# One-token attention and a gated MLP on one core: result, gate and pieces of x as eight neighbouring rows, and wo's last four rows through masked stationary tiles

## The chip, the cores and the metric

The kernel runs on one core of a Trainium2 chip. The metric is the device time of one execution in microseconds (us); smaller is better. Of several executions the median is given.

## The reference

Two tokens (B = 2, one position each, D = 512) go through an attention block with a cached K and V, and through an MLP whose output gates the attention's:

```
xn = _layernorm(x, axis=-1)
q = (xn @ wq).reshape(B, 1, 32, 128).transpose(0, 2, 1, 3)
scores = einsum("bhqd,bhkd->bhqk", q, k_cache) * 128 ** -0.5     # 8192 keys
o = einsum("bhqk,bhkd->bhqd", softmax(scores), v_cache)
s = o.transpose(0, 2, 1, 3).reshape(B, 1, 4096) @ wo
h = _gelu(_layernorm(xn) @ w1 + b1)                              # 512 -> 1376
g = _silu(h @ w2 + b2)                                           # 1376 -> 512
out = x + s * g
```

Everything is float32. K and V are 268 MB each; wq and wo have 8.4 MB each, w1 and w2 2.8 MB each.

## The kernel before

Each engine runs its own program, written out in the order of the code, with semaphores between them. The helper `op` (line 51) records nearly every instruction, so the profile shows L51 for nearly all. Names such as `bank` and `big` stand for all of PSUM's eight banks and for the three large SBUF buffers; most of the weights of the setup lie in the third of these.

**Transfers.** SP issues almost all of them on one queue: w2's tail, w1, wq, the first K tile, w2, the second K tile, x as `x4`, the first V tile, then K and V tiles in turn (32 pairs of 8.4 MB tiles). The first V tile overwrites the setup's weights, so SP waits for the setup's last matmul (`pgate`, line 304) ahead of it. At the end `wo` comes into the last V buffer in seven pieces (`WO_CUTS`: wo rows 0-9, 10-17, 18-23, 24-27, 28-29, 30 and 31, where a "row" c is one [128, 512] block), the last of them in two halves of the columns.

**Loop.** For each of the 32 tiles VectorE (DVE) multiplies K by q and sums, ScalarE (ACT) makes the exponentials, and TensorE (PE) multiplies them with V. Some matmuls with `ident` (the helper `unread`) write results that nobody reads.

**The end.** The normalised attention output lies in `on`: column c of it, for the B = 2 tokens, is the stationary operand for row c of wo. In the kernel before `on` is [128, 17, 32], zero except in the entries 0 and 16 of the 17, so that a matmul writes 17 neighbouring partitions and the two tokens come 16 partitions apart. Rows 0 to 27 are "wide": all 512 columns in one matmul, with c modulo 4 choosing one of four strips of 32 PSUM partitions in `pw`. ACT then copies `pw` to `o4`, and four matmuls with `mod` (a 0/1 matrix) add the four strips into `acc`. Rows 28 to 31 go straight into `acc`: the 512 columns are cut into QT = 4 quarters of 128, and quarter j goes to the strip 32j of `acc`, with one matmul per row and quarter. So `acc`, `gate`, `x4` and `res` are [128, 128], with useful rows at 32j + 16b. DVE makes `res = 0.5 * acc * gate + x4` in two instructions, and SP writes `res` out from eight partitions, 16 apart. PE reaches the rows in the order 0 to 29, then the four matmuls with `mod`, then 30 and 31.

In the setup, four matmuls (`pgate`) bring the gate's input into the same layout, with `mod_b` as the stationary tile and one strip for each quarter. `pqa` is another part of the setup that the prediction speaks of: eight matmuls with 64 stationary columns each and 128 moving columns, all into the same 64 partitions of one bank.

Of the kernel before, what the change touches and what calls it, by code (L numbers as in the profile page):

```python
# [5 lines left out]
ALU = mybir.AluOpType  # L6
# [7 lines left out]
class Program:  # L14
# [32 lines left out]
    def op(self, eng, method, *args, waits=(), sig=None, by=1, quiet=False, **kwargs):  # L47
        need = self.need(eng, waits)
        for name, v in need[:-1]:
            self.engines[eng].wait_ge(self.sem(name), v)  # L50
        ins = getattr(self.engines[eng], method)(*args, **kwargs)  # L51
        for name, v in need[-1:]:
            ins._wait_ge(self.sem(name), v)
        if quiet:
            return None
        name = sig or "own_" + eng
        by = 16 if method == "dma_start" else by
        ins.then_inc(self.sem(name), by)
        self.counts[name] += by
        return name, self.counts[name]  # L60


def decode_kernel(nc, x, kc, vc, wq, wo, w1, b1, w2, b2, out):
    P = 128
    B, H, S, DH = kc.shape
# [10 lines left out]
    SCALE = float(DH) ** -0.5  # L76
    QT = 4
    R = P // QT
    HB = R // B
    MB = HB * (B - 1) + 1  # L80
    JW = 512 // DH
    NT = KP // JW
    NF = F // P
# [3 lines left out]
    OC = DH // PH  # L87
# [4 lines left out]
    WIDE = 28  # L92
# [3 lines left out]
    op, wait, take = pr.op, pr.wait, pr.take  # L96

    def sb(shape, name):
        return nc.alloc_sbuf_tensor(name, list(shape), F32).ap()
# [30 lines left out]
    g_nat = boot(P, D)  # L130
    wq_sb = big[1].rearrange("p (c n) -> p c n", n=H * DH)
    wo_sb = big[2].rearrange("p (c n) -> p c n", n=D)
# [6 lines left out]
    mod = sb([P, R], "mod")  # L139
# [3 lines left out]
    mine = sb([BH, N], "mine")  # L143
    side = sb([BH, U], "side")
    sides = sb([BH, P], "sides")
    x4 = sb([P, P], "x4")
    gate = sb([P, P], "gate")
    res = sb([P, P], "res")
    z = sb([P, P], "z")
    th = sb([P, P], "th")  # L150
    xnT = sb([P, ND, B], "xnT")
    yT = sb([P, ND, B], "yT")
    hT = sb([P, NF + 1, B], "hT")
# [8 lines left out]
    o4 = sb([P, JW * DH], "o4")  # L162
# [1 line left out]
    Z = sb([P, BH, PH], "Z")  # L164
    ZL = sb([P, N, U * PH], "ZL")
    rl = sb([P, B], "rl")
    on = sb([P, MB, OC], "on")
    mod_b = sb([P, R], "mod_b")

    bank = [ps([P, 512], f"bank{i}") for i in range(8)]  # L170
    po = bank[0]
    pm = bank[1]
    pn = bank[2]
    pt = bank[3]
    acc = bank[4][:, :P]
    OA = bank[5][:, :B * (OC + 1)].rearrange("p (b c) -> p b c", c=OC + 1)
    pg = bank[6]
    pw = bank[1]
    ph = bank[7][:, :NH * P]
    pgate = bank[7][:, :P]  # L180
    phT = bank[3][:, R:R + (NF + 1) * B]
    PQ = [bank[1], bank[2]]
    pxn, py = bank[3][:, :ND * B], bank[5][:, :ND * B]
# [9 lines left out]
    def pe_n(name, n):  # L193
        return name, n + 1

    t = {}
# [19 lines left out]
    a = op("POOL", "memset", ident, 0.0)  # L216
# [2 lines left out]
    t["sel0"] = op("POOL", "memset", sel, 0.0)  # L219
    op("POOL", "memset", PZ, 0.0)  # L220
    op("POOL", "memset", srow, SCALE)
    t["x4m"] = op("POOL", "memset", x4, 0.0)
    t["on0"] = op("POOL", "memset", on, 0.0)
    a = op("POOL", "memset", mod_b, 0.0)
    t["pool"] = op("POOL", "memset", gate, 0.0)
    op("DVE", "memset", eps_t, EPS)
    for k in (7, 6, 1, 2, 4, 0):
        t[f"mem{k}"] = t["mem"] = op("DVE", "memset", bank[k], 0.0)
# [3 lines left out]
    a = op("DVE", "tensor_reduce", out=side, in_=pairs.rearrange("h n s -> h s n"), axis=AX.X, op=ALU.add)  # L232
    t["side"] = op("DVE", "tensor_copy", sides.rearrange("h (s r) -> h s r", r=HP),
                   side.unsqueeze(2).to_broadcast([BH, U, HP]), waits=[a])
    a = op("DVE", "tensor_reduce", out=half1, in_=ident.rearrange("p (s r) -> p s r", s=U), axis=AX.X, op=ALU.add)
    t["half"] = op("DVE", "tensor_copy", half.rearrange("p (s r) -> p s r", r=PH),
                   half1.unsqueeze(2).to_broadcast([P, U, PH]), waits=[a])
    t["mod"] = op("DVE", "tensor_reduce", out=mod, in_=by_row, axis=AX.X, op=ALU.add, waits=[t["ident"]])
    t["mod_b"] = op("DVE", "tensor_copy", mod_b[:, ::HB], mod[:, :B], waits=[t["mod"], t["pool"]])
    t["blk"] = op("DVE", "tensor_reduce", out=blk, in_=ident.rearrange("p (j r) -> p j r", r=R), axis=AX.X,  # L240
                  op=ALU.add)
    t["sel"] = op("DVE", "tensor_copy",
                  sel[:, HP:].rearrange("p (b j r) -> p b j r", b=B, r=HG)[:, :, :QT, 0], by_row[:, :B, :],
                  waits=[t["sel0"]])
# [22 lines left out]
    a = op("DVE", "tensor_copy", gh, phT.rearrange("p (f b) -> p f b", b=B), waits=[pe("phT")])  # L267
    c = op("DVE", "tensor_mul", gu, gh, gh, waits=[a])
    c = op("DVE", "tensor_scalar", gu, gu, GELU_A, 1.0, op0=ALU.mult, op1=ALU.add, waits=[c])
    c = op("DVE", "tensor_mul", gu, gu, gh, waits=[c])  # L270
    c = op("ACT", "activation", gu, gu, AF.Tanh, scale=GELU_C, waits=[c])
    c = op("DVE", "scalar_tensor_tensor", gu, gu, 1.0, gh, op0=ALU.add, op1=ALU.mult, waits=[c])
# [8 lines left out]
    for part, n0, n1 in (("first", 0, NPB), ("rest", NPB, N)):  # L281
        shape = [BH, n1 - n0, DH]
        t[f"QN {part}"] = op("DVE", "tensor_tensor", out=QN[:, n0:n1, :], in0=q_all.unsqueeze(1).to_broadcast(shape),
                           in1=mine[:, n0:n1].unsqueeze(2).to_broadcast(shape), op=ALU.mult,
                           waits=[t["qall"], t["mine"]])

    for g in range(N // NPB):
        last = {"sig": "s_q", "by": NPB // U * (2 if g == QH + 1 else 1)} if g != QH else {}
# [7 lines left out]


    load_k(1, pe("pq"), ("d_wq", 16))
    for b in range(B):
        t["x4"] = op("SP", "dma_start", x4[HB * b::R, :], x[b, 0].rearrange("(j n) -> j n", n=P), sig="d_x4",  # L300
                     waits=[t["x4m"]])


    wait("SP", t["sel"], t["qnat"], pe(PE_EVENTS[-1]))
# [37 lines left out]
    with nc.scalar.Fori(0, N // U) as i:  # L342
        for u in range(U):
# [4 lines left out]
            for s in range(U):  # L348
                r = slice(HP * s, HP * (s + 1))
# [6 lines left out]
    t["OT"] = "a_ot", N  # L356

    t["gate"] = op("DVE", "scalar_tensor_tensor", gate, th, 1.0, z, op0=ALU.add, op1=ALU.mult,
                   waits=[t["th"], t["pool"]])
    shape = [P, N, U * PH]  # L360
    t["ZL"] = op("DVE", "tensor_tensor", out=ZL, in0=half.unsqueeze(1).to_broadcast(shape),
                 in1=RS.unsqueeze(2).to_broadcast(shape), op=ALU.mult, waits=[pe_n("p_z", 0), t["half"]])
    t["rl"] = op("DVE", "reciprocal", rl, OA[:, :, OC], waits=[pe_n("p_den", 0)])
    shape = [P, BH, PH]
    t["Z"] = op("DVE", "tensor_tensor", out=Z, in0=blk.unsqueeze(1).to_broadcast(shape),
                in1=OT.unsqueeze(2).to_broadcast(shape), op=ALU.mult, waits=[t["OT"], t["blk"]])
    t["on"] = op("DVE", "tensor_tensor", out=on[:, ::HB, :], in0=OA[:, :, :OC], in1=rl.unsqueeze(2).to_broadcast([P, B, OC]),
                 op=ALU.mult, waits=[t["rl"], t["on0"], pe_n("p_oa", 0)])
    t["wide"] = op("ACT", "copy", o4, pw, waits=[pe_n("p_w", 0)])
    a = op("DVE", "scalar_tensor_tensor", res, acc, 0.5, gate, op0=ALU.mult, op1=ALU.mult,  # L370
           waits=[pe_n("p_acc", 0), t["gate"]])
    t["res"] = op("DVE", "tensor_add", res, res, x4, waits=[a, t["x4"]])
    t["out"] = op("SP", "dma_start", out.rearrange("b s (j n) -> j (b s) n", n=P), res[::HB, :], sig="d_out",
                  waits=[t["res"]])
    wait("SP", t["out"])

# [4 lines left out]
    def mm(dst, w, v, start=True, stop=True, sig=None, waits=(), skip=False):  # L381
        kw = {"skip_group_check": True} if skip else {}
        if sig in PE_EVENTS:
            done.append(sig)
            sig = "pe_setup"
        return op("PE", "matmul", dst, w, v, start=start, stop=stop, waits=waits, sig=sig, quiet=sig is None, **kw)
# [15 lines left out]
    for c in range(ND):  # L402
        for j in range(QT):
            w = w1_v[:, c, j:NF:QT, :]
            mm(ph[R * j:R * j + B, :w.shape[1] * P].rearrange("b (f p) -> b f p", p=P), yT[:, c, :], w,
               start=c == 0, stop=False, waits=[t["yT"], t["mem7"], ("d_w1", 16)])
        j, k = NF % QT, NF // QT
        mm(ph[R * j:R * j + B, k * P:k * P + FT], yT[:, c, :], w1_sb[:, c, NF * P:], start=False, stop=False)
    b1_v = b1_sb[:, :NF * P].rearrange("o (p f) -> o f p", f=NF)
    for j in range(QT):  # L410
        w = b1_v[:, j:NF:QT, :]
        mm(ph[R * j:R * j + B, :w.shape[1] * P].rearrange("b (f p) -> b f p", p=P), ones[:1, :B], w,
           start=False, stop=j != NF % QT, waits=[t["b1"]])
    j, k = NF % QT, NF // QT
    mm(ph[R * j:R * j + B, k * P:k * P + FT], ones[:1, :B], b1_sb[:, NF * P:], start=False, stop=True, sig="ph")
    by_tile = ident.rearrange("p (j r) -> p j r", r=R)
    for k in range(NH):
        n = min(QT, NF + 1 - k * QT)
        mm(phT[:, k * QT * B:(k * QT + n) * B].rearrange("p (j b) -> p j b", b=B), h_nat[:, k * P:(k + 1) * P],
           by_tile[:, :n, :B], waits=[t["h"]], sig="phT" if k == NH - 1 else None)  # L420
    for n in range(NG // QT):
        for c in range(ND):
            for j in range(QT):
                g = n * QT + j
                last = n == NG // QT - 1 and c == ND - 1 and j == QT - 1
                mm(PQ[n][R * j:R * j + B, :], xnT[:, c, :], wq_sb[:, c, g * 512:(g + 1) * 512], start=c == 0,
                   stop=c == ND - 1, waits=[t["xnT"], t["mem"], ("d_wq", 16)], sig="pq" if last else None)
    for n in range(NG // QT):
        for hh in range(HG):
            a = HP - (n * QT * HG + hh)  # L430
            last = n == NG // QT - 1 and hh == HG - 1
            mm(pqa[:BH, :], sel[:, a:a + BH], q_nat[:, n, hh * DH:(hh + 1) * DH], start=n + hh == 0, stop=last,
               waits=[t["sel"], t["qnat"]], sig="pqa" if last else None)

    for g in range(N // NPB):
        mm(PB[g % len(PB)], sides, QN[:, g * NPB:(g + 1) * NPB, :].rearrange("h n d -> h (n d)"),
           waits=[t["side"], t["QN rest" if g else "QN first"]] + ([t[f"Q{QH}"]] if g >= len(PB) else []),
           sig=f"pb{g}")
    for f in range(NF + 1):
        j = f % QT  # L440
        k = P if f < NF else FT
        mm(pg[R * j:R * j + B, :], hT[:k, f, :], w2_sb[:k, f, :], start=f < QT, stop=f + QT > NF and j != QT - 1,
           waits=[t["hT"], t["w2"], t["mem6"]])
    mm(pg[R * (QT - 1):R * (QT - 1) + B, :], ones[:1, :B], b2_sb, start=False, stop=True, waits=[t["b2"]], sig="pg")
    for j in range(QT):
        mm(pgate[R * j:R * j + MB, :], mod_b[:, :MB], g_nat[:, j * P:(j + 1) * P], waits=[t["g"], t["mod_b"]],
           sig="pgate" if j == QT - 1 else None)
    assert done == PE_EVENTS, done

    def unread(*heads):  # L450
# [65 lines left out]
    unread(1)  # L516
    for i, (c0, c1) in enumerate(zip(WO_CUTS, WO_CUTS[1:])):
        for c in range(c0, c1):
            after = [t["on"], t["mem"], (f"d_wo{i}", 16)]
            if c < WIDE:  # L520
                j = c % QT
                mm(pw[R * j:R * j + MB, :], on[:, :, c], wo_sb[:, c, :], start=c < QT, stop=c + QT >= WIDE,
                   waits=after, sig="p_w" if c == WIDE - 1 else None)
                continue
            for j in range(QT):
                last = c == OC - 1 and j == QT - 1
                if c == OC - 1 and j * P >= LAST_COLS[1]:
                    after = [("d_wol", 16)]
                mm(acc[R * j:R * j + MB, :], on[:, :, c], wo_sb[:, c, j * P:(j + 1) * P], start=c == WIDE,
                   stop=c == OC - 1, waits=after, sig="p_acc" if last else None)  # L530
        if c1 == OC - 2:
            for j in range(QT):
                mm(acc[R * j:R * j + MB, :], mod[:, :MB], o4[:, j * P:(j + 1) * P], start=False, stop=False,
                   waits=[t["wide"]])


# [24 lines left out]
```

## Time and profile before

| | |
|---|---|
| median of 3 runs | 1300.24 us (1300.05 to 1301.04) |
| span of the profiled execution | 1298.7 us |
| run's median less that span | 1.5 us |
| moved from HBM | 559.3 MB, 431 GB/s |
| PE busy | 461.9 us, 36% |
| DVE busy | 1135.7 us, 87% |
| ACT busy | 72.0 us, 6% |
| mean share of TensorE's full clock granted | 0.679 |

The span runs from the first to the last instruction of one profiled execution; no other time is given of that execution, and what lies around the span is taken as the 1.5 us between it and the median. A float32 matmul of the code stands in the trace as two records, each with its own load of the stationary tile (LDWEIGHTS, on the row PEld).

### The profile page before, as it was taken

The numbers are of one execution on the slowest core, as the hardware profiler recorded it, in microseconds if no ns is written. First come the engines' busy times: TensorE is split into PE (matmuls) and PEld (weight loads), VectorE is DVE, ScalarE is ACT, GpSimd is POOL, SyncE is SP. The second block draws the span as 40 slices with busy tenths as digits, with TensorE's granted clock in tenths as the row PEclk, the third lists the DMA queues.
The fourth block names the chain that finished last, engine by engine and source line by source line (L and its number), as shares of the span: only waits on it lengthen the run. The fifth ranks groups of instructions, "written<-read, shape, count | busy, mean of one in ns | idle before, by whom it ended". The sixth has DMA issues, their size and how long they took to land. (4 is left out here: it accounts for less than half of the span.)

```text
span 1298.7 us, 7184 instructions
## 1 busy us (share of the span) xinstructions
PE 461.9 (36%) x2958; PEld 148.9 (11%) x2958; DVE 1135.7 (87%) x171; ACT 72.0 (6%) x245; POOL 2.1 (0%) x14
## 2 busy tenths in 40 slices
PE   3813434322433322343322344322334321333337
PEld 1201111001111000111000111100111100111103
DVE  2599999988889988889988888988888988888991
ACT  1100000000000000000000000000000000000000
POOL 0000000000000000000000000000000000000000
PEclk8756776667777567777556767656776666677659
DMA  9999999999999999999999999999999999999998
GB/s 412 436 426 444 424 440 430 426 446 424 444 426 430 440 426 446 424 442 426 426 446 426 444 426 438 430 426 446 426 444 424 438 432 426 446 424 442 416 432 360
DMA packets 11242, 559.38 MB, mean 431 GB/s; under 512 B 1264, under 2 KB 1536, under 8 KB 1892
## 3 DMA queue, kind: packets, MB, share of 16 engines
q1 hardware_dynamic: 11228, 559.30, 99.7%
q8 instruction: 3, 0.05, 0.0%
q14 instruction: 3, 0.02, 0.0%
q10 hardware_dynamic: 8, 0.01, 0.0%
HBM read 559.30 MB, written 0.00 MB: 431 GB/s over the span
## 5 line engine op out<-in xcount | busy, mean ns | idle before, releaser
L51 DVE TENSOR_TENSOR big<-big,Q 128x16384 f32<-128x16384 f32 (+1 forms) x33 | 551.3, 16707 | 73.5 <-DVEq L45 73.5
L51 DVE TENSOR_REDUCE sc<-big 128x128 f32<-128x16384 f32 (+1 forms) x33 | 551.2, 16703 | 4.8
L51 PE MATMUL bank<-big,PZ 128*8 128x512 f32 x2048 | 292.5, 735 | 629.2 <-PEq L45 629.2
L51 PEld LDWEIGHTS bank<-big,PZ 128*8 128x8 f32 x2048 | 60.5, 103 | 833.8 <-issue 833.8
L51 PE MATMUL bank<-Q,ident 128*128 128x512 f32 (+2 forms) x198 | 78.6, 507 | 0.2 <-issue 0.2
L51 ACT COPY o<-bank 128x512 f32<-128x512 f32 x33 | 19.3, 585 | 893.3 <-ACTq L45 881.7
L51 PE MATMUL bank<-ident,MX 128*1 128x128 f32 x32 | 9.2, 286 | 136.7 <-PEq L45 136.7
L51 PE MATMUL bank<-mod,o 128*128 128x2 f32 x256 | 32.8, 250 | 27.4 <-PEq L45 27.4
L51 PEld LDWEIGHTS bank<-mod,o 128*128 128x128 f32 x256 | 31.0, 191 | 55.4 <-issue 55.4
L51 PEld LDWEIGHTS bank<-Q,ident 128*128 128x128 f32 x198 | 33.6, 197 | 16.5 <-issue 16.5
L51 ACT ACTIVATE PZ<-sc,bias 64x128 f32<-64x128 f32 x64 | 25.5, 399 | 6.6 <-ACTq L45 6.2
L51 DVE TENSOR_REDUCE nm<-bank 1x2 f32<-1x128 f32 x32 | 8.9, 279 | 18.8 <-DVEq L45 18.8
L51 DVE TENSOR_TENSOR big<-big,mine 64x512 f32<-64x512 f32 (+1 forms) x2 | 4.5, 2279 | 21.8 <-ACT big L51 21.8
L51 PEld LDWEIGHTS bank<-ident,MX 128*1 128x1 f32 x32 | 2.5, 79 | 161.7 <-issue 161.7
L51 ACT COPY bias<-bank 128x1 f32<-128x1 f32 x32 | 5.1, 159 | 223.6 <-ACTq L45 223.6
L51 PE MATMUL bank<-big,sides 64*128 64x512 f32 x16 | 12.6, 962 | 3.7 <-DVE big L51 3.7
L51 PE MATMUL bank<-nm,srow 1*64 1x1 f32 x128 | 10.2, 216 | 9.8 <-PEq L45 9.4
L51 DVE TENSOR_REDUCE MX<-sc 128x1 f32<-128x128 f32 x32 | 9.2, 286 | 4.7
L51 PE MATMUL bank<-big,xnT 128*2 128x512 f32 x64 | 9.2, 744 | 10.6 <-DMA big<-in_A_wq_dram 10.6
L51 ACT ACTIVATION_READ_ACCUMULATOR PZ<-sc,bias x64 | 11.8, 185 | 0.0
L51 DVE SCALAR_TENSOR_TENSOR res<-bank,gate 128x128 f32<-128x128 f32 x1 | 0.3, 292 | 12.1 <-PE bank L51 12.1
L51 PEld LDWEIGHTS bank<-nm,srow 1*64 1x64 f32 x128 | 8.5, 160 | 16.1 <-issue 16.1
(78 smaller groups left out, 74.7 us busy)
## 6 DMA issues: line engine op xcount, KB each, us to landing
big<-in_A_k_cache_dram SPq DMA_DIRECT2D x2, 4096.0 KB, 35.9
big<-in_A_v_cache_dram SPq DMA_DIRECT2D x2, 4096.0 KB, 36.0
big<-in_B_w_dram SPq DMA_DIRECT2D x1, 2752.0 KB, 10.3
big<-in_B_w_dram SPq DMA_DIRECT2D x1, 2560.0 KB, 52.4
big<-in_A_wo_dram SPq DMA_DIRECT2D x1, 2560.0 KB, 14.9
big<-in_A_wo_dram SPq DMA_DIRECT2D x1, 2048.0 KB, 19.4
big<-in_A_wo_dram SPq DMA_DIRECT2D x1, 1536.0 KB, 22.6
big<-in_A_wo_dram SPq DMA_DIRECT2D x1, 1024.0 KB, 24.3
```

Source lines behind the costliest of these rows:

```text
L51: ins = getattr(self.engines[eng], method)(*args, **kwargs)
```

## The change

`x4`, `gate`, `res`, `z`, `th` and `acc` become [8, 128]: partition 4b + j holds quarter j of token b. x comes in one transfer of eight rows instead of two of four, without a wait for a memset, and the result goes out from eight neighbouring partitions.

Since the quarters now share a strip, quarter j of a row must write only its own partitions. For this the stationary tile has eight columns, of which two are not zero: `onr` holds such a tile for each of the last four rows and each quarter, and `modr` one for each quarter in place of `mod_b` and `mod`. A matmul with a masked tile adds zero to the other six partitions. All sixteen matmuls of rows 28 to 31, the four with `modr` between them, and the four of `pgate` write the same eight partitions. `on` shrinks to [128, 2, 32], so wide matmuls have 2 stationary columns instead of 17. DVE fills `onr` by two copies after `on`, and every matmul with wo waits for the second of them.

```diff
-    x4 = sb([P, P], "x4")
-    gate = sb([P, P], "gate")
-    res = sb([P, P], "res")
+    x4 = sb([OR, P], "x4")
+    gate = sb([OR, P], "gate")
+    res = sb([OR, P], "res")
...
-    on = sb([P, MB, OC], "on")
-    mod_b = sb([P, R], "mod_b")
+    on = sb([P, B, OC], "on")
+    onr = sb([P, (OC - WIDE) * QT * OS], "onr")
+    modr = sb([P, QT * OS], "modr")
...
-    acc = bank[4][:, :P]
+    acc = bank[4][:OR, :P]
...
-    for b in range(B):
-        t["x4"] = op("SP", "dma_start", x4[HB * b::R, :], x[b, 0].rearrange("(j n) -> j n", n=P), sig="d_x4",
-                     waits=[t["x4m"]])
+    t["x4"] = op("SP", "dma_start", x4, x.rearrange("b s (j n) -> (b s j) n", n=P), sig="d_x4")
...
+    onr_v = onr.rearrange("p (c j r) -> p c j r", j=QT, r=OS)
+    for b in range(B):
+        shape = [P, OC - WIDE, QT]
+        t["onr"] = op("DVE", "tensor_copy", onr_v[:, :, :, b * QT], on[:, b, WIDE:].unsqueeze(2).to_broadcast(shape),
+                      waits=[t["on"], t["pool"]])
...
-        mm(pgate[R * j:R * j + MB, :], mod_b[:, :MB], g_nat[:, j * P:(j + 1) * P], waits=[t["g"], t["mod_b"]],
-           sig="pgate" if j == QT - 1 else None)
+        mm(pgate, modr[:, j * OR:(j + 1) * OR], g_nat[:, j * P:(j + 1) * P], start=j == 0, stop=j == QT - 1,
+           waits=[t["g"], t["modr"]], sig="pgate" if j == QT - 1 else None)
...
-            after = [t["on"], t["mem"], (f"d_wo{i}", 16)]
+            after = [t["onr"], t["mem"], (f"d_wo{i}", 16)]
...
-                mm(acc[R * j:R * j + MB, :], on[:, :, c], wo_sb[:, c, j * P:(j + 1) * P], start=c == WIDE,
-                   stop=c == OC - 1, waits=after, sig="p_acc" if last else None)
+                r = (c - WIDE) * QT * OS + j * OR
+                mm(acc, onr[:, r:r + OR], wo_sb[:, c, j * P:(j + 1) * P], start=c == WIDE and j == 0,
+                   stop=last, waits=after, sig="p_acc" if last else None)
```

On PE the end of the program stood like this, from the last wide matmuls on (`d_wo4` to `d_wol` are the landings of wo's last pieces; a row gives stationary columns by moving columns):

```order
L51 MATMUL bank<-big,on 17x512 [waits d_wo3]
L51 MATMUL bank<-big,on 17x512 x3
L51 MATMUL bank<-big,on 17x128 [waits d_wo4]
L51 MATMUL bank<-big,on 17x128 x7
L51 MATMUL bank<-o,mod 17x128 [waits own_ACT]
L51 MATMUL bank<-o,mod 17x128 x3
L51 MATMUL bank<-big,on 17x128 [waits d_wo5]
L51 MATMUL bank<-big,on 17x128 x3
L51 MATMUL bank<-big,on 17x128 [waits d_wo6]
L51 MATMUL bank<-big,on 17x128
L51 MATMUL bank<-big,on 17x128 [waits d_wol]
L51 MATMUL bank<-big,on 17x128
```

The same place of the changed program:

```order
L51 MATMUL bank<-big,on 2x512 [waits d_wo3]
L51 MATMUL bank<-big,on 2x512 x3
L51 MATMUL bank<-big,onr 8x128 [waits d_wo4]
L51 MATMUL bank<-big,onr 8x128 x7
L51 MATMUL bank<-o,modr 8x128 [waits own_ACT]
L51 MATMUL bank<-o,modr 8x128 x3
L51 MATMUL bank<-big,onr 8x128 [waits d_wo5]
L51 MATMUL bank<-big,onr 8x128 x3
L51 MATMUL bank<-big,onr 8x128 [waits d_wo6]
L51 MATMUL bank<-big,onr 8x128
L51 MATMUL bank<-big,onr 8x128 [waits d_wol]
L51 MATMUL bank<-big,onr 8x128
```

No matmul moved, none came or went, and the waits are the same; the stationary tiles became narrower, and the rows do not show that the 20 matmuls of 128 columns no longer go to four strips.

On DVE the last instructions of the program, as a difference between the two:

```order
 L51 TENSOR_TENSOR Z<-blk,OT 128x256
-L51 TENSOR_TENSOR on<-bank,rl 128x2x32
-L51 SCALAR_TENSOR_TENSOR res<-bank,gate 128x128
-L51 TENSOR_TENSOR res<-res,x 128x128
+L51 TENSOR_TENSOR on<-bank,rl 128x64
+L51 COPY onr<-on 128x16 x2
+L51 SCALAR_TENSOR_TENSOR res<-bank,gate 8x128
+L51 TENSOR_TENSOR res<-res,x 8x128
```

Two copies stand new between `on` and the last two instructions, which keep their 128 elements per partition and lose 120 of their partitions.

## Rows read from the trace of the kernel before

**Rows 1.** The page's slices: busy tenths in 40 equal parts of the span.

```profile
DVE  2599999988889988889988888988888988888991
PEclk8756776667777567777556767656776666677659
DMA  9999999999999999999999999999999999999998
```

**Rows 2.** The chain that ended last, its end: start us, us, what.

```profile
1269.32 25.18 DMA big<-in_A_wo_dram
1294.50 0.04 issue
1294.54 1.68 PE bank L51 x40
1296.22 0.02 issue
1296.25 0.30 DVE res L51
...
1296.64 0.29 DVE res L51
```

**Rows 3.** Timeline of the end: start us, us, engine, instruction xcount [idle before <-releaser].

```profile
1283.94 0.23 DVE L51 TENSOR_TENSOR on<-bank,rl 128x64 f32<-128x64 f32 x1 [0.72 <-PE bank L51]
1284.31 4.65 PE L51 MATMUL bank<-big,on 128*17 128x512 f32 x36
1290.73 1.92 PE L51 MATMUL bank<-big,on 128*17 128x512 f32 x12 [1.77 <-DMA big<-in_A_wo_dram]
1294.40 0.60 ACT L51 COPY o<-bank 128x512 f32<-128x512 f32 x1 [11.64 <-PE bank L51]
1294.54 0.66 PE L51 MATMUL bank<-big,on 128*17 128x128 f32 x16 [0.19 <-DMA big<-in_A_wo_dram]
1295.78 0.15 PEld L51 LDWEIGHTS bank<-big,on 128*17 128x17 f32 x4 [0.17 <-DMA big<-in_A_wo_dram]
1296.96 0.61 SPq L51 DMA_DIRECT2D out_dram<-res  x1
```

**Rows 4.** Groups by shape, setup's `pqa` matmuls and their loads: busy us, mean ns.

```profile
L51 PE MATMUL bank<-big 128*64 128x128 f32 x16 | 2.0, 276 | 1.2 <-ACT big L51 1.2
L51 PEld LDWEIGHTS bank<-big 128*64 128x64 f32 x16 | 1.7, 137 | 2.1 <-ACT big L51 2.1
```

**Rows 5.** Timeline of the same matmuls, whole and from a later start.

```profile
41.76 1.96 PE L51 MATMUL bank<-big 128*64 128x128 f32 x16 [1.20 <-ACT big L51]
...
42.69 1.04 PE L51 MATMUL bank<-big 128*64 128x128 f32 x8
```

**Rows 6.** Windows: stretch, PE, PEld, DVE, ACT, POOL busy us, granted clock, DMA share, GB/s.

```profile
12.00:18.00 6.00, 5.78 (x44) 2.28 (x48) 0.07 (x1) 0.00 (x0) 0.00 (x0) 1.00 1.10 472
35.00:40.60 5.60, 5.56 (x48) 1.00 (x40) 0.00 (x0) 0.00 (x0) 0.00 (x0) 0.93 0.94 410
41.70:43.80 2.10, 1.96 (x16) 1.72 (x16) 0.00 (x0) 0.05 (x2) 0.00 (x0) 1.00 1.15 499
48.50:60.00 11.50, 11.41 (x14) 4.16 (x14) 9.18 (x2) 3.51 (x6) 0.00 (x0) 0.54 1.09 468
1284.00:1296.00 12.00, 9.33 (x98) 3.00 (x97) 0.17 (x1) 0.60 (x1) 0.00 (x0) 1.00 0.84 343
```

**Rows 7.** Timeline: small DVE copies, ACT copies, and the setup's `pgate` stretch.

```profile
4.37 0.22 DVE L51 COPY sides<-side 64x128 f32<-64x128 f32 x1
...
4.82 0.17 DVE L51 COPY half<-half 128x8 f32<-128x8 f32 x1
...
43.76 0.26 ACT L51 COPY big<-bank 64x128 f32<-64x128 f32 x1 [2.05 <-PE bank L51]
...
65.90 0.41 PE L51 MATMUL bank<-big,mod_b 128*17 128x128 f32 x8 [0.67 <-ACT big L51]
66.38 0.27 ACT L51 COPY z<-bank 128x128 f32<-128x128 f32 x1 [0.53 <-PE bank L51]
```

**Rows 8.** Timeline of SP in the setup.

```profile
40.70 0.33 SPq L51 DMA_DIRECT2D big<-in_A_k_cache_dram  x1
41.07 1.23 SPq L51 DMA_DIRECT2D x<-in_A_x_dram  x2
66.43 0.33 SPq L51 DMA_DIRECT2D big<-in_A_v_cache_dram  x1
```

**Rows 9.** DMA issues, the second K tile alone: KB, us from issue to landing.

```profile
big<-in_A_k_cache_dram SPq DMA_DIRECT2D x1, 35.4
```

**Rows 10.** Loads of the last V tiles, at either clock: start us, us.

```profile
1259.22 0.17 PEld L51 LDWEIGHTS bank<-big,PZ 128*8 128x8 f32 x4 [0.69 <-issue]
1260.08 0.17 PEld L51 LDWEIGHTS bank<-big,PZ 128*8 128x8 f32 x4 [0.69 <-issue]
...
1263.20 0.10 PEld L51 LDWEIGHTS bank<-big,PZ 128*8 128x8 f32 x4 [0.33 <-issue]
1263.63 0.10 PEld L51 LDWEIGHTS bank<-big,PZ 128*8 128x8 f32 x4 [0.33 <-issue]
```

More of the change, by code (lines that the diff above doesn't have):

```diff
@@ L78, in decode_kernel @@
     R = P // QT
-    HB = R // B
-    MB = HB * (B - 1) + 1
+    OR = B * QT
+    OS = OR + 1
     JW = 512 // DH
@@ L145, in decode_kernel @@
     sides = sb([BH, P], "sides")
-    x4 = sb([P, P], "x4")
-    gate = sb([P, P], "gate")
-    res = sb([P, P], "res")
-    z = sb([P, P], "z")
-    th = sb([P, P], "th")
+    x4 = sb([OR, P], "x4")
+    gate = sb([OR, P], "gate")
+    res = sb([OR, P], "res")
+    z = sb([OR, P], "z")
+    th = sb([OR, P], "th")
     xnT = sb([P, ND, B], "xnT")
@@ L179, in decode_kernel @@
     ph = bank[7][:, :NH * P]
-    pgate = bank[7][:, :P]
+    pgate = bank[7][:OR, :P]
     phT = bank[3][:, R:R + (NF + 1) * B]
@@ L221, in decode_kernel @@
     op("POOL", "memset", srow, SCALE)
[L222 to L225, printed above, removed]
+    op("POOL", "memset", onr, 0.0)
+    t["pool"] = op("POOL", "memset", modr, 0.0)
     op("DVE", "memset", eps_t, EPS)
@@ L238, in decode_kernel @@
     t["mod"] = op("DVE", "tensor_reduce", out=mod, in_=by_row, axis=AX.X, op=ALU.add, waits=[t["ident"]])
-    t["mod_b"] = op("DVE", "tensor_copy", mod_b[:, ::HB], mod[:, :B], waits=[t["mod"], t["pool"]])
+    t["modr"] = op("DVE", "tensor_copy", modr.rearrange("p (j r) -> p j r", r=OS)[:, :, :OR:QT],
+                   mod[:, :B].unsqueeze(1).to_broadcast([P, QT, B]), waits=[t["mod"], t["pool"]])
     t["blk"] = op("DVE", "tensor_reduce", out=blk, in_=ident.rearrange("p (j r) -> p j r", r=R), axis=AX.X,
@@ L358, in decode_kernel @@
     t["gate"] = op("DVE", "scalar_tensor_tensor", gate, th, 1.0, z, op0=ALU.add, op1=ALU.mult,
-                   waits=[t["th"], t["pool"]])
+                   waits=[t["th"]])
     shape = [P, N, U * PH]
@@ L366, in decode_kernel @@
                 in1=OT.unsqueeze(2).to_broadcast(shape), op=ALU.mult, waits=[t["OT"], t["blk"]])
-    t["on"] = op("DVE", "tensor_tensor", out=on[:, ::HB, :], in0=OA[:, :, :OC], in1=rl.unsqueeze(2).to_broadcast([P, B, OC]),
-                 op=ALU.mult, waits=[t["rl"], t["on0"], pe_n("p_oa", 0)])
+    t["on"] = op("DVE", "tensor_tensor", out=on, in0=OA[:, :, :OC], in1=rl.unsqueeze(2).to_broadcast([P, B, OC]),
+                 op=ALU.mult, waits=[t["rl"], pe_n("p_oa", 0)])
+    onr_v = onr.rearrange("p (c j r) -> p c j r", j=QT, r=OS)
[3 more added lines that the diff above has]
+                      waits=[t["on"], t["pool"]])
     t["wide"] = op("ACT", "copy", o4, pw, waits=[pe_n("p_w", 0)])
@@ L372, in decode_kernel @@
     t["res"] = op("DVE", "tensor_add", res, res, x4, waits=[a, t["x4"]])
-    t["out"] = op("SP", "dma_start", out.rearrange("b s (j n) -> j (b s) n", n=P), res[::HB, :], sig="d_out",
+    t["out"] = op("SP", "dma_start", out.rearrange("b s (j n) -> (b s j) n", n=P), res, sig="d_out",
                   waits=[t["res"]])
@@ L518, in decode_kernel @@
         for c in range(c0, c1):
-            after = [t["on"], t["mem"], (f"d_wo{i}", 16)]
+            after = [t["onr"], t["mem"], (f"d_wo{i}", 16)]
             if c < WIDE:
                 j = c % QT
-                mm(pw[R * j:R * j + MB, :], on[:, :, c], wo_sb[:, c, :], start=c < QT, stop=c + QT >= WIDE,
+                mm(pw[R * j:R * j + B, :], on[:, :, c], wo_sb[:, c, :], start=c < QT, stop=c + QT >= WIDE,
                    waits=after, sig="p_w" if c == WIDE - 1 else None)
@@ L528, in decode_kernel @@
                     after = [("d_wol", 16)]
-                mm(acc[R * j:R * j + MB, :], on[:, :, c], wo_sb[:, c, j * P:(j + 1) * P], start=c == WIDE,
-                   stop=c == OC - 1, waits=after, sig="p_acc" if last else None)
+                r = (c - WIDE) * QT * OS + j * OR
+                mm(acc, onr[:, r:r + OR], wo_sb[:, c, j * P:(j + 1) * P], start=c == WIDE and j == 0,
+                   stop=last, waits=after, sig="p_acc" if last else None)
         if c1 == OC - 2:
             for j in range(QT):
-                mm(acc[R * j:R * j + MB, :], mod[:, :MB], o4[:, j * P:(j + 1) * P], start=False, stop=False,
+                mm(acc, modr[:, j * OR:(j + 1) * OR], o4[:, j * P:(j + 1) * P], start=False, stop=False,
                    waits=[t["wide"]])
```

## The prediction

> **What bounds the kernel now.** I began with the page's slices [rows 1]. The DMA line stands at 9 in all but the last of 40 slices while PE's clock moves between its levels and DVE is at 8 or 9: the transfer stream is never out of work, so no engine's duration matters before the stream has run dry. Then I read the end of the chain of waits [rows 2]. It goes back from the last DVE instruction to one stretch of 40 matmul records, and from there to a transfer of wo that lands at 1294.50 us. Whatever this change does to the time, it does in the 4.2 us from there to the end of the span at 1298.7, or by making the stream start something later.
>
> The timeline of the end [rows 3] shows that stretch. The last four rows of wo land close together. At 1294.54 the first 16 records (eight matmuls: rows 28 and 29) start, and all 16 together take 0.66 us. At 1295.78 a load of a stationary tile starts that had waited 0.17 us for a transfer: that is the last half row, so now PE keeps up with the landings and the last piece ends the wait. The records are over at 1296.22 [rows 2], DVE needs two instructions of 0.29 to 0.30 us, and SP issues the output at 1296.96 for 0.61 us [rows 3].
>
> **The 20 narrow matmuls.** Rows 28 to 31 are 16 matmuls of 128 moving columns, the merging of `o4` is four more: 20 matmuls, 40 records. Before, the four quarters of a row went to four strips of PSUM partitions. After, all 20 accumulate into partitions 0 to 7, that is, into one strip. What does a matmul of 128 columns cost when it follows others into the same partitions, each with its own stationary tile? The setup has just this: `pqa`, eight matmuls, 16 records, at clock 1.00 [rows 6]. They take 1.96 us, with a mean record of 276 ns [rows 4, 5]. Records overlap, so the step from one start to the next is (1.96 - 0.28) / 15 = 0.112 us; from the later eight alone, which are free of the first load, (1.04 - 0.28) / 7 = 0.109 us. In the old end 16 records need only (0.66 - 0.28) / 15 = 0.025 us per step, so there four are under way at once. This is the one difference that I expect to see.
>
> Worked out: 39 steps of 0.109 us are 4.25 us (0.112: 4.37), and the last record's own 0.28 us comes on top. From 1294.54 that gives an end at 1299.07 to 1299.19, where the old one was 1296.22. I take the faster step, since the new tiles have 8 columns where those of `pqa` have 64, and add 0.03 us for the first load: **2.9 us later**, with 2.85 and 3.0 as the bounds of this row. The lower bound beyond it is the old step: the tiles overlap as the strips do, and the end stays where it is, 0.
>
> All pieces of wo will have landed by 1295.78, when PE has done about 11 of its 40 records; from then on PE waits for nothing but itself. The wait for the last transfer vanishes, and what is late next is `res`.
>
> A rule that would make it worse: by the Trainium skill, "TensorE: Matmul & The Clock Gate", Part 3 on packing small matmuls, a stationary load overlaps matmuls in flight only when it goes to other row groups; the same page also allows a background weight buffer. All loads here use all 128 rows. In the trace the `pqa` loads use all 128 rows too, their records take 137 ns each, and 16 of them with 16 matmuls fit into 1.96 us [rows 4, 5]; if load and matmul went in turn it would be 16 x (0.109 + 0.137) = 3.9 us. The trace disagrees with that sentence, so loads cost nothing here; by the rule the sum would be 40 x 0.137 = 5.5 us more.
>
> **The chain behind them.** The two DVE instructions and the output lose partitions, not elements per partition. ACT's copies of 128 elements took 0.26 us on 64 partitions and 0.27 on 128 [rows 7], so I take 0 for them. The output has eight pieces of 512 bytes before and after; SP took 0.61 us for its issue, the x transfers of four pieces took 1.23 / 2 = 0.61 each, large transfers 0.33 [rows 3, 8]. Bounds: 0, or 0.28 us saved; it is nearest to the small ones, so 0.
>
> **The copies into `onr`.** `on` ends at 1284.17. Small DVE copies took 0.17 to 0.22 us [rows 7]; with 0.04 us between instructions two end near 1284.65, and every matmul with wo now waits for them, so PE starts about 0.5 us after its old 1284.31. Its first stretch of 36 records then ends near 1289.5 instead of 1288.96, and the next piece lets it go on at 1290.73 after an idle time of 1.77 us [rows 3]. That idle time is the cover, 1.3 us of it remain, and the cost is 0; without it, it would be 0.5 us. ACT's copy of `pw` ends at 1295.00 [rows 3]; PE now comes to the matmuls that need it after 16 steps, at 1296.3, so that wait is gone.
>
> **The setup.** `pgate`'s eight records took 0.41 us [rows 7] and become 7 x 0.109 + 0.28 = 1.04, so SP issues the first V tile 0.6 us later than at 66.43 [rows 8]. The cover is the second K tile, issued at 40.70 and landed 35.4 us later [rows 8, 9], at 76.1: the stream has 9 us of work when V is appended. Cost 0; without the cover 0.6 us. SP's one issue less for x (0.61 us) is spent in a stretch in which SP waits for `pgate` anyway: 0. Fewer memsets on the idle POOL, and one wider copy on DVE in the first 6 us, end long before wq has landed: 0. The loop is the same.
>
> **Sum.** Span 1298.7 + 2.9 = 1301.6 us; the run's median is 1.5 us above the span, so 1303.1 us, 0.22% over 1300.24. The measured runs lie up to 0.8 us from their median, and 0.2% (2.6 us) is about what a measurement of this kernel can tell from no change: the forecast sits just past it.
>
> **Rivals.**
>
> *The masked tiles overlap after all* (not slower). For it: the tiles are narrower, and the array does run four such matmuls at once now. Against it: `pqa`'s records, which share partitions, keep 0.109 us apart. PE would end at 1296.2 as before, and at best the issue of the output saves 0.28: 1300.0 to 1300.2 us. The point from which it decides is a step of 0.10 us: 39 x 0.101 + 0.28 from 1294.54 ends at 1298.8, 2.6 us late. A gain over 0.2% has no place in the end, since only 3 us lie behind the last landing; it would need a faster stream, for which no row speaks.
>
> *The clock falls in the long narrow stretch.* At the lower of the two levels, 1.2 GHz, everything doubles: the loads of V's tiles stood 0.86 us apart under it and 0.43 us when it had risen [rows 10]. For it: one strip is busy where four were, and between 48.5 and 60 us a PE busy for 11.41 of 11.50 us had 0.54 [rows 6], with stationary tiles that cover only half of the rows. Against it: the new tiles use all 128 rows, matmuls with two stationary columns had 1.00 and 0.93 (12 to 18 and 35 to 40.6 us), `pqa` kept 1.00, and the old end had 1.00 throughout although PE had gaps of over 1 us [rows 3, 6]. If it falls halfway, 20 steps cost 0.109 more each: 1303.1 + 2.2 = 1305.3 us; from the start, 1307.4.
>
> *Load and matmul in turn*: 1303.1 + 5.5 = 1308.6 us, if the step is 0.25 instead of 0.109. The rule is that of the page named above; `pqa` speaks against it.
>
> *Less is serial than I think*: the gain in SP's issue is real and the step is a little under 0.109, or the landings come later than in this execution, which leaves less of the old tail to lose: 2.0 to 2.6 us, so 1302.2 to 1302.8. Nothing in the rows tells this from the forecast but their scatter.
>
> **How the numbers follow.** One strip, in sequence, at the full clock: 0.75, and that case includes the variant with a little less. Of it I put 0.53 past 2.6 us and 0.22 under, as the centre is 2.9 and bounds and scatter of the median are some 0.5 us together. The clock falls: 0.10, slower. Load and matmul in turn: 0.02, slower. Overlap: 0.08, within 0.2%. Something that no row shows: 0.05, split between faster (0.04) and same. Slower 0.65, same 0.31, faster 0.04. The range from 1301.8 to 1304.9 holds the first case nearly whole (0.73) and most of the falls that come late (0.07).
>
> **What would show it.** In the new trace the 16 + 8 + 16 records from rows 28 to 31 should start about 0.109 us apart and make one stretch of some 4.5 us without a wait for a transfer; the chain should go from the last landing that starts this stretch (rows 28 and 29) through about 4.5 us of PE to `res`. The two copies should stand between `on` and a PE start near 1284.8, followed by an idle time before 1290.7 that is still there. `pgate` should take about 1.0 us, and the landing of the first V tile should stay. I am wrong if the records of one quarter start inside those of another (then nothing is lost), if the granted clock is 0.5 anywhere after 1284, or if the wide matmuls reach row 28 later than its landing.

## The result, and the profile after

| | before | after |
|---|---|---|
| median of 21 runs | 1300.05 us (1299.65 to 1301.40) | 1302.45 us (1302.11 to 1303.22) |
| span of the profiled execution | 1298.7 us | 1300.8 us |
| ratio | | 1.0019, 95% interval 1.0013 to 1.0024 |

The changed kernel is 2.4 us slower. That is just inside the 0.2% (2.6 us) that the prediction drew as its bound, and the interval reaches past it.

The end of the chain of waits of the kernel after (start us, us, what) answers to [rows 2]:

```profile
1269.32 24.91 DMA big<-in_A_wo_dram
1294.22 0.04 issue
1294.27 4.55 PE bank L51 x40
1298.81 0.02 issue
1298.84 0.29 DVE res L51
...
1299.22 0.28 DVE res L51
```

The chain has the same members. The 40 records behind the landing of wo's rows 28 and 29 last 4.55 us, where they lasted 1.68 [rows 2]. The timeline of the same stretch, answering to [rows 3]:

```profile
1283.77 0.23 DVE L51 TENSOR_TENSOR on<-bank,rl 128x64 f32<-128x64 f32 x1 [0.72 <-PE bank L51]
1284.03 0.26 DVE L51 COPY onr<-on 128x16 f32<-128x16 f32 x2
1284.44 4.46 PE L51 MATMUL bank<-big,on 128*2 128x512 f32 x36 [0.40 <-DVE onr L51]
...
1290.50 1.89 PE L51 MATMUL bank<-big,on 128*2 128x512 f32 x12 [1.60 <-DMA big<-in_A_wo_dram]
...
1294.27 1.91 PE L51 MATMUL bank<-big,onr 128*8 128x128 f32 x16 [0.24 <-DMA big<-in_A_wo_dram]
...
1296.02 1.04 PE L51 MATMUL bank<-o,modr 128*8 128x128 f32 x8
...
1296.89 1.91 PE L51 MATMUL bank<-big,onr 128*8 128x128 f32 x16
...
1299.53 0.31 SPq L51 DMA_DIRECT2D out_dram<-res  x1
```

The first sixteen records take 1.91 us instead of 0.66, and behind the first of them no record of the 40 waits for a transfer any more. Two more rows show smaller things. At 1284.44 PE has waited 0.40 us for the copies into `onr`, of which nothing is left at 1290.50, since PE waits there for a piece of wo anyway. In the last row the issue of the output takes 0.31 us where it took 0.61 [rows 3].

The groups by shape of that stretch (count, busy us, mean ns):

```profile
L51 PE MATMUL bank<-big,onr 128*8 128x128 f32 x32 | 3.8, 273 | 0.2 <-DMA big<-in_A_wo_dram 0.2
L51 PEld LDWEIGHTS bank<-big,onr 128*8 128x8 f32 x32 | 2.8, 90 | 1.7 <-DMA big<-in_A_wo_dram 1.2
```

and its window (us, busy of PE, PEld, DVE, ACT, POOL, granted clock, DMA share, GB/s):

```profile
1284.00:1298.80 14.80, 11.96 (x97) 5.03 (x96) 0.26 (x2) 0.58 (x1) 0.00 (x0) 1.00 0.67 272
```

A single record is as long as before, 273 ns against the 276 of `pqa` [rows 4]; it is their spacing that grew: (4.55 - 0.27) / 39 = 0.110 us. The granted clock was 1.00 to the end.

In the setup, SP's rows answer to [rows 8], and the `pgate` row among them to [rows 7]:

```profile
40.59 0.33 SPq L51 DMA_DIRECT2D big<-in_A_k_cache_dram  x1
40.97 0.38 SPq L51 DMA_DIRECT2D x<-in_A_x_dram  x1
...
66.31 1.04 PE L51 MATMUL bank<-big,modr 128*8 128x128 f32 x8 [0.68 <-ACT big L51]
...
67.44 0.34 SPq L51 DMA_DIRECT2D big<-in_A_v_cache_dram  x1
```

The first V tile is issued 1.0 us later than before, and x needs 0.38 us of SP instead of 1.23. Of the 1.0 us, `pgate` made 0.63 (1.04 us instead of 0.41); the rest is that it began 0.41 us later in this execution, and in the other runs with the changed setup it began anywhere from 65.3 to 67.2. The landing of the first V tile did not move: 66.43 + 29.0 = 95.4 us before and 67.44 + 27.7 = 95.1 after, by these rows (us from issue to landing; before, then after):

```profile
big<-in_A_v_cache_dram SPq DMA_DIRECT2D x1, 29.0
...
big<-in_A_v_cache_dram SPq DMA_DIRECT2D x1, 27.7
```

**Where the 2.4 us are.** From the landing of rows 28 and 29 to the end of PE it was 1296.22 - 1294.50 = 1.72 us and is 1298.81 - 1294.22 = 4.59: 2.87 more. From the start of the output's issue to the end of the span it was 1298.7 - 1296.96 = 1.74 us and is 1300.8 - 1299.53 = 1.27: 0.47 less. DVE's part between the two gave 0.02 us. Together 2.38 us, and the medians differ by 2.40. The profiled spans differ by only 2.1, since in this one execution that landing came 0.28 us earlier.

### The profile page after: what moved, and what is told of

Its sections match the earlier page's. It is cut to its first block, busy times and chain, and to the rows that moved or that the text cites. A ratio compares the mean times of both kernels' runs of the same rounds, so it can differ in the third digit from the quotient of the medians.

```text
span 1300.8 us, 7183 instructions
## 1 busy us (share of the span) xinstructions
PE 461.9 (36%) x2958; PEld 151.8 (12%) x2958; DVE 1135.9 (87%) x173; ACT 71.9 (6%) x245; POOL 1.4 (0%) x12
## 5 line engine op out<-in xcount | busy, mean ns | idle before, releaser
L51 PE MATMUL bank<-big,PZ 128*8 128x512 f32 x2048 | 287.5, 724 | 628.4 <-PEq L45 628.4
```

## The experiments

The theory: matmuls into the same strip of 32 PSUM partitions run one after the other, 0.109 us per record, whichever tile they use; the output in one plain transfer from neighbouring partitions gives 0.45 us back. The rivals are named with each run. Each was timed beside runs of the kernel before on its chip, whose medians were 1300.02 to 1300.11 us.

**Strips again, all else as changed.**

```diff
+    strips = [bank[4][R * j:R * j + OR, :P] for j in range(QT)]
...
-                mm(acc, onr[:, r:r + OR], wo_sb[:, c, j * P:(j + 1) * P], start=c == WIDE and j == 0,
-                   stop=last, waits=after, sig="p_acc" if last else None)
+                mm(strips[j], onr[:, r:r + OR], wo_sb[:, c, j * P:(j + 1) * P], start=c == WIDE,
+                   stop=c == OC - 1, waits=after, sig="p_acc" if last else None)
...
-                mm(acc, modr[:, j * OR:(j + 1) * OR], o4[:, j * P:(j + 1) * P], start=False, stop=False,
+                mm(strips[j], modr[:, j * OR:(j + 1) * OR], o4[:, j * P:(j + 1) * P], start=False, stop=False,
```

> The changed kernel, but quarter j of the last four rows, and of the merging of o4, goes again to its own strip 32j of the bank; DVE still reads the first eight partitions, so the sums of quarters 1 to 3 are left out of the result. Same tiles of eight columns, same 20 matmuls, same output transfer. If sharing one strip is what costs (my theory): the records of four quarters run inside one another again, the stretch behind the landing of rows 28 and 29 falls from 4.55 us to about 1.7, and the time is 1302.45 - 2.85 = 1299.6 us. If the masked tiles themselves, or their number, cost: about 1302.4 us.

Measured: 1299.42 us (11 runs), 3.0 us under the changed kernel. Chain and output of this kernel:

```profile
1294.65 0.04 issue
1294.70 1.72 PE bank L51 x40
1296.41 0.02 issue
...
1297.13 0.31 SPq L51 DMA_DIRECT2D out_dram<-res  x1
```

The same 40 records with the same tiles of eight columns last 1.72 us as soon as their outputs lie in four strips, so neither the tiles nor their number cost. Against the kernel before the ratio is 0.9995 (0.9986 to 1.0004): with the strips and the cheap output it is at most a little faster, and it is no candidate, since the sums of quarters 1 to 3 are missing from its result.

**Twice the narrow matmuls, in the same strip or in the next.** The two kernels differ in the region alone:

```diff
+    spare = bank[6][:OR, :P]          # in the other kernel: bank[6][R:R + OR, :P]
...
+                if not last:
+                    mm(spare, onr[:, r:r + OR], wo_sb[:, c, j * P:(j + 1) * P], waits=after)
...
+                mm(spare, modr[:, j * OR:(j + 1) * OR], o4[:, j * P:(j + 1) * P], waits=[t["wide"]])
```

> The changed kernel with 19 more matmuls of 128 columns, one ahead of each narrow one (save the last), with the same operands, into partitions 0 to 7 of another bank. If the strip is what is shared, a different bank does not help: 19 x 2 x 0.109 = 4.1 us more, 1306.6 us. Rival: the matmuls wait for one another because they add to the same addresses of PSUM; then those of the other bank fit between them and the time stays within 0.5 us of 1302.45.

> As the run with 19 more matmuls, but these go to partitions 32 to 39 of the other bank, the second strip. If the strip is what is shared: each extra matmul runs beside its neighbour, and the time stays at 1302.5 us, within 0.3. If the number of matmuls and loads sets the pace: 1306.6 us as in the run with the same strip.

Measured: 1306.42 us with the same strip, 1302.16 with the other. The chains, first of the kernel with the same strip:

```profile
1294.35 0.04 issue
1294.39 8.70 PE bank L51 x78
```

and of the kernel with the other strip:

```profile
1294.16 0.04 issue
1294.20 4.55 PE bank L51 x78
```

The extra matmuls read the same operands in the same order in both. With another bank but the same partitions, 38 more records cost 8.70 - 4.55 = 4.15 us, 0.109 each; in partitions 32 to 39 they cost nothing. So it is neither the addresses nor the bank of the sum that serialises, but the strip. All outputs that had to wait here lay in the same eight partitions; that other partitions of the same 32 would wait as well was not tried. By the Trainium skill ("TensorE: Matmul & The Clock Gate", Part 3, "What picks the tile position") the column tile follows from the partition at which the output starts; these two runs agree, with 8.70 us from partition 0 and 4.55 from partition 32.

**The output alone, in the kernel before.**

```diff
-    t["out"] = op("SP", "dma_start", out.rearrange("b s (j n) -> j (b s) n", n=P), res[::HB, :], sig="d_out",
+    t["out"] = op("SP", "dma_start", out.rearrange("b s (j n) -> (b s j) n", n=P), res[:B * QT, :], sig="d_out",
```

> The kernel before, with the output taken from partitions 0 to 7 of its result tile in one plain [8, 128] transfer (seven of the eight rows are then not the result). Theory: the changed kernel lost 2.87 us on TensorE but got 0.45 us back, since the output transfer took 1.26 us from issue to its end instead of 1.71; so here 1300.05 - 0.45 = 1299.6 us and an issue of 0.31 us instead of 0.61. Rival: the output's gain was chance of the profiled execution or belongs to the changed DVE work; then 1300.0 and an issue of 0.6.

Measured: 1300.08 us (1299.14 to 1300.97), ratio 1.0001 (0.9992 to 1.0010). The timeline of this kernel, whose span is 1297.8 us:

```profile
1296.56 0.32 SPq L51 DMA_DIRECT2D out_dram<-res  x1
```

The issue fell as expected and the output's part is 1297.8 - 1296.56 = 1.24 us, but the time did not follow. The spans did in part: their median over the 11 runs is 1298.2 us against 1298.5 for the kernel before. The difference lies outside the span: in 6 of the 11 runs time and span are 1.3 us apart, in 5 of them 2.0 to 2.5. Such runs occur with the kernel before as well (3 of 27), and why there are more here stays open.

**The changed kernel with the output in the other order.**

```diff
-    t["out"] = op("SP", "dma_start", out.rearrange("b s (j n) -> (b s j) n", n=P), res, sig="d_out",
+    t["out"] = op("SP", "dma_start", out.rearrange("b s (j n) -> j (b s) n", n=P), res, sig="d_out",
```

> The changed kernel with its eight result rows written in the other order (quarter first, as the kernel before did), still from partitions 0 to 7; the result's rows come in the wrong order. If the cheap issue needs both neighbouring partitions and a plain order of the rows, this issue takes 0.5 to 0.7 us instead of 0.31, and the output's part of the end is about 1.7 us again instead of 1.27: 1302.45 + 0.45 = 1302.9 us. If it is only the neighbouring partitions: 1302.45 us and 0.31. The run with the plain output in the kernel before left open whether the 0.45 us reaches the time at all, as its times scatter by 1.8 us; if it does not: 1302.45 us in spite of a dear issue.

Measured: 1302.78 us, ratio 1.0023 (1.0014 to 1.0032), span 1301.3 us:

```profile
1299.34 0.76 SPq L51 DMA_DIRECT2D out_dram<-res  x1
```

The issue became dear, 0.76 us, and the output's part 1301.3 - 1299.34 = 1.96 us, although the partitions are neighbours: the plain order is needed too. In the time it is 0.33 us, in the expected direction, but its interval overlaps that of the changed kernel. The spans of all timed executions lie closer to the traces: their median is 1301.4 us here and 1301.0 for the changed kernel, 1298.2 for the kernel before with the plain output and 1298.5 beside it. So the gain is 0.3 to 0.5 us within the span, and is not shown in the times.

**What an issue costs by its shape.**

```diff
+    t["step16"] = op("SP", "dma_start", sb([P, P], "step16")[::16, :], x.rearrange("b s (j n) -> (b s j) n", n=P), sig="d_step16")
+    t["near4"] = op("SP", "dma_start", sb([P, P], "near4")[:4, :], x.rearrange("b s (j n) -> (b s j) n", n=P)[:4], sig="d_near4")
+    t["step32"] = op("SP", "dma_start", sb([P, P], "step32")[::32, :], x.rearrange("b s (j n) -> (b s j) n", n=P)[:4], sig="d_step32")
+    t["swap8"] = op("SP", "dma_start", sb([P, P], "swap8")[:8, :], x.rearrange("b s (j n) -> j (b s) n", n=P), sig="d_swap8")
+    t["swap16"] = op("SP", "dma_start", sb([P, P], "swap16")[::16, :], x.rearrange("b s (j n) -> j (b s) n", n=P), sig="d_swap16")
...
+    wait("SP", t["step16"], t["near4"], t["step32"], t["swap8"], t["swap16"])
```

> The changed kernel with five more small transfers of x on SP behind x4, each into a tile of its own that nobody reads, to see what an issue costs by its shape. All are pieces of 512 bytes. If it is partitions that are not neighbours which make the issue dear: eight rows 16 apart and four rows 32 apart take about 0.6 us each, four neighbours and eight neighbours about 0.3 to 0.4, also with the rows of x taken in the other order (quarter first). If it is a pattern of two levels in x: both with the other order take 0.6, and the rows 16 and 32 apart in plain order 0.3. The run's time stays at 1302.45 within 0.5 us, since SP waits there for the gate anyway.

Measured: 1302.22 us, one run. SP's timeline, in the order of the diff behind x4's own issue:

```profile
40.95 0.38 SPq L51 DMA_DIRECT2D x<-in_A_x_dram  x1
41.38 0.69 SPq L51 DMA_DIRECT2D step<-in_A_x_dram  x1
42.11 0.46 SPq L51 DMA_DIRECT2D near<-in_A_x_dram  x1
42.61 0.54 SPq L51 DMA_DIRECT2D step<-in_A_x_dram  x1
43.20 1.25 SPq L51 DMA_DIRECT2D swap<-in_A_x_dram  x2
...
43.91 0.53 SPq L51 DMA_DIRECT2D swap<-in_A_x_dram  x1
```

The last row is the second of the two in the row above it, taken from a later start; the first of them takes 0.67. Eight neighbours in plain order are cheapest (0.38). Rows 16 apart make the issue 0.69, the other order 0.67, and both together 0.53, so either alone makes it dearer and the two do not add up. For four rows the distance costs less: 0.46 for neighbours, 0.54 for rows 32 apart. So neither explanation alone holds. One record of each does not give a finer price; at the output the other order alone cost 0.76 - 0.31 = 0.45 us.

**More wide rows, fewer masked ones.** Two kernels:

```diff
-    WIDE = 28
+    WIDE = 30          # in the other kernel: 31
...
-        if c1 == OC - 2:
+        if c1 == OC - 1:          # in the other kernel: OC
```

In the other kernel the last matmul of the merging, and not of row 31, also closes the sum and signals DVE.

> The changed kernel with rows 28 and 29 wide as well (four strips), and the merging of o4 behind row 30: 12 matmuls instead of 20 in the one strip. By the strip theory PE has, after the landing of rows 28 and 29, 0.85 us of wide matmuls and then 24 records of 0.109: end of PE 0.87 us earlier, about 1301.6 us. If the length of the stretch in one strip does not set the end: 1302.45. If the merging now waits for ACT's copy of pw, which starts after row 29 instead of row 27: up to 0.5 us of the gain is lost.

> The changed kernel with rows 28 to 30 wide and only row 31 through masked tiles, the merging of o4 last: 8 matmuls in the one strip. The wide part then ends some 1.05 us after row 30 lands, ACT's copy takes 0.6 us, the merging 8 records of 0.109 and 0.17 us: a PE end about 2.75 us after row 30's landing, where it was 3.96 in the changed kernel: 1.2 us less, 1301.2 us. If the copy and the merging cost more behind the wide part than the strip does: no gain against 1301.6 of the run with 12.

Measured: 1301.32 us with 30 wide rows and 1300.96 with 31. The chains, first of 30:

```profile
1294.04 0.04 issue
1294.09 3.65 PE bank L51 x28
```

and of 31:

```profile
1294.34 1.65 PE bank L51 x7
1295.99 0.02 issue
1296.02 0.59 ACT o L51
1296.61 0.04 issue
1296.65 1.05 PE bank L51 x8
1297.71 0.02 issue
```

Each masked matmul taken out of the strip gives time back: 4.55 us of PE become 3.65 with 12 of them, 0.90 less where 0.87 was expected, and the time fell by 1.1. With 31 wide rows it is no longer the matmuls of wo's rows that set the end, but ACT's copy and the four merging matmuls behind it. These still share the one strip: their eight records take 1.05 us, where `pgate`'s eight took 0.41 in four strips [rows 7]. That is the best full version with the new layout, 1.5 us faster than the change, and not faster than the kernel before: ratio 1.0006 (0.9997 to 1.0015). No run here beats the kernel before clear of the noise.

**A later first V tile.**

```diff
+    for j in range(64):
+        mm(bank[7][:OR, 3 * P:], modr[:, :OR], g_nat[:, :P], waits=[t["g"], t["modr"]])
```

> The changed kernel with 64 more narrow matmuls ahead of pgate, into a part of its bank that nobody reads: 64 x 0.218 = 14 us, so that SP issues the first V tile at 81.4 us instead of 67.4. I hold that the setup's longer pgate costs nothing because the second K tile keeps the stream busy until 75.8 us. Then the stream runs dry for 5.6 us, and a little longer until the new transfer delivers: 1308 to 1310 us. If the stream had no such need of the first V tile (rival): 1302.45.

Measured: 1312.12 us, 9.7 us above the changed kernel and outside what I expected. SP's timeline in this kernel:

```profile
82.32 0.34 SPq L51 DMA_DIRECT2D big<-in_A_v_cache_dram  x1
```

and two of its windows (the last two columns are the DMA share and GB/s):

```profile
70.00:75.00 5.00, 5.00 (x49) 4.12 (x47) 5.00 (x1) 0.00 (x0) 0.00 (x0) 1.00 0.59 253
75.00:80.00 5.00, 5.00 (x49) 4.12 (x47) 5.00 (x1) 0.00 (x0) 0.00 (x0) 1.00 0.00 0
```

The issue came 82.32 - 67.44 = 14.9 us later and 9.7 us were lost (four runs), so about 5.2 us were covered: V had to be issued by about 67.44 + 5.2 = 72.6. I had read the cover off the landing of the second K tile, 76.1 us (76.7 in this kernel). But that is the landing of its last part: the trace has one landing for each of 16 parts, and 11 of them lie between 73.8 and 74.5 us. The windows show no more than a share of 0.59 from 70 to 75 us, and none behind it. And V's first packets start only at 83.3, 1.0 us after their issue. The change's delay of 1.0 us is still well inside the cover.

## Why the prediction held, point by point

- *The narrow matmuls run in sequence, 2.9 us.* Right in mechanism and size: 2.87 us, at 0.110 us per record. `pqa` gave the price to within 0.001 us, although its tiles have 64 columns and these have 8. The three runs with strips and doubled matmuls show that the strip is the cause.
- *The chain behind them, 0.* Mis-sized: this is the term that made the total 2.4 instead of 2.9. I had bounds of 0 and 0.28 us for the output's issue and took 0 because it is as small as x's old transfers. But these too had rows 32 apart; their equal 0.61 us was no evidence that small transfers are dear. (Distance alone does not explain the 0.61 either: in the run by shape four rows 32 apart took 0.54 and four neighbours 0.46.) The output's part fell by 0.47 us, 0.30 of it in the issue and the rest behind it, which the bound of 0.28 had left out. DVE's two instructions changed by 0.01 us each, as taken. The forecast time of 1303.1 us stood another 0.2 us higher because it began from the 1300.24 of three runs, where 21 runs gave 1300.05.
- *The copies into `onr`, 0.* Right. Together they took 0.26 us, less than the 0.48 that I had put; PE started 0.67 us after `on` did, instead of 0.37, and the idle time before the next piece fell from 1.77 to 1.60 us.
- *The setup, 0.* Right: `pgate` took the 1.04 us that the sum gave, and the landing of the first V tile stayed. The cover was overstated: 9 us by the landing, 5 to 6 by the run with a late V tile.
- *The clock falling in the narrow stretch* did not happen: 1.00 from 1284 us on, also in the 8.70 us of the doubled run. *Load and matmul in turn* did not happen either: the step is the same 0.11 us with these loads of 90 ns as with `pqa`'s of 137 (with loads of 90 ns that rival's price would have been 3.6 us, and not 5.5). The trace disagrees with the sentence of the Trainium skill that was weighed ahead of the run ("TensorE: Matmul & The Clock Gate", Part 3, "What overlaps and what doesn't"). *Overlap after all* is refuted by the chain.
- *The chances.* 0.65 stood on slower by over 0.2%; the time fell 0.2 us short of that, into the 0.31 for no change by that bound, and into what the rivals called less serial than thought (2.0 to 2.6 us). Of the reasons named there only the gain in SP's issue came true; the step was not under 0.109, and the landings did not come later.

## What to carry to other kernels

In these runs four matmuls with few stationary columns ran beside one another when their outputs lay in different strips of 32 partitions, and in sequence when they lay in the same eight partitions. Merging outputs onto neighbouring partitions with masked tiles keeps the arithmetic right, but here it took the step from 0.025 to 0.110 us and the stretch from 1.68 to 4.55 us, and at the end of a kernel, behind the last transfer, nothing hides it. The tidy layout earned 0.3 to 0.5 us of the span at the output, so compare such a gain with the number of narrow matmuls behind the last landing. And do not take the time at which a stream needs its next transfer from the landing of the transfer before: in the run with a late V tile it was some 4 us earlier.

## What the runs showed of the hardware

- A transfer of eight 512-byte rows took SP 0.31 to 0.38 us to issue when the partitions are neighbours and the rows in plain order, and 0.53 to 0.76 us otherwise; from the start of the issue to the end of the span the output took 1.23 to 1.30 us in the first case and 1.74 to 1.96 in the others.
- Nineteen more matmuls in a second strip, with their own loads, cost nothing measurable: 78 records in the 4.55 us of 40.
- Time and span differ by 1.3 to 1.6 us in most executions and by 1.9 to 2.5 us in some, in this kernel's case enough to hide a gain of 0.3 us.
